# Plain pair of the second network: earlier weight loads, six split buffers, an even spread of the output layer and of the token work

## The chip, the cores and the metric

The kernel runs on one core of one Trainium2 chip. The metric is the device time of one execution, in microseconds (us). A core has five engines, each with its own in-order instruction stream: PE (matmul; PEld is its weight load), DVE (vector), ACT (scalar, reads PSUM), POOL (GpSimd, cannot read PSUM) and SP, which here only issues DMAs. A DMA waits on SP for its own conditions, and everything queued behind it on SP waits too.

## The reference

Three stages follow each other: a WKV recurrence over 768 steps (4 batches, 8 heads of 48), a first network and a second network. The change lies in the second one and at its border to the first:

```
# x: 3072 tokens x 384, from the recurrence
h = x @ w_in                              # 384 -> 2048
x = (h * clip(h + 3, 0, 6) / 6) @ w_out   # first network, 2048 -> 384
rms = sqrt(mean(x * x, axis=-1) + 1e-6)
xn = x / rms * rms_g
g = xn @ w_gate                           # second network, 384 -> 1536
silu = g / (1 + exp(-g))
return (silu * (xn @ w_val)) @ w_out      # 1536 -> 384
```

## The kernel before

The 3072 tokens are cut into six chunks of 512. The first network runs chunk by chunk, 16 steps of 128 hidden features each (`steps`); the recurrence and the preparation of weights run beside it. Each chunk's normalised result goes to DRAM (`xn`). The second network takes the chunks as three **pairs** p = 0, 1, 2. Its 1536 hidden features are four groups of 3 x 128; each group takes two **periods**, one for the gate and one for the value, so a pair has eight periods and the loop variable `j` runs from 0 to 24 (24 flushes). `p, k = divmod(j, 8)`.

Every fp32 factor is split into a high and a low fp32r part (copy on ACT, subtraction on POOL or DVE), and every product is three matmuls of 128x512 (`triple`, line 729 before, 730 after the change): high-high, high-low, low-high. Such a threesome is called a **unit** below, and the order of all engines' instructions is pinned to the order in which the program writes them (`pin`).

Pair 0 is the **plain pair** (`Plain`, j = 0 to 7): 18 units a period, three per hidden tile, with the weights `wp` that are loaded into two slots (`slots[0]` is the tile `w0`, printed as `w`; `slots[1]` is the front of `wide_b`). The other two pairs (`Triple`) form the 3x3 by 3x2 block product with 15 products in place of 18, from combinations of weights (`wd`) and of tokens. Both kinds of combination are made beside the plain pair, as **chores** placed at unit counts: `Group.sums` adds weight planes (DVE, line 226), `Group.split` splits five pieces per group into `chl` buffers (ACT line 249, POOL line 250) and stores them to DRAM as `wd`; `Combined.add` forms token combinations (`xc`, POOL line 693) and `Combined.split` splits them into their homes in `wide_a` and `wide_b` (`part`, ACT line 711, POOL or DVE line 712). For pair 2 the token work runs inside the last three periods of pair 1 and the first of pair 2, through the queue `after(n, ...)`, which runs a function n units later.

In a gate period ACT writes silu; in a value period DVE (plain) or POOL (`Triple`; for the product e6 DVE) multiplies with the gate (`done`, lines 826 and 829) and ACT and POOL split the result for the output layer (lines 834 and 835, tiles `xt` and `g`). The output layer's units (`out_units`, nine per chunk and group, result `o`) are a list `fill` that is interleaved with the period's own units; in `Triple` periods the letter F of `FULL` takes one. PSUM results of the plain pair rotate over four banks (`pa`, `pc`, `pe`, `pb`).

SP's stream before: `load_wp(0)` stands after the first network, `load_wp(j + 1)` at the start of period j, `load_wo` (output weights) in odd periods, `load_wc`/`load_we` (the combined weights, in two parts) for pairs 1 and 2, and between them the `wd` stores and the loads of `planes`.

Of the kernel before, what the change touches and what calls it, by code (L numbers as in the profile page):

```python
# [10 lines left out]
F32R = mybir.dt.float32r  # L11
# [24 lines left out]
def kernel(  # L36
# [171 lines left out]
    class Group:  # L208
# [36 lines left out]
        def split(self, b):  # L245
            hl = pl_p.tile([128, 2 * DM], F32R, tag="hl", name="chl", bufs=3)
            h = hl.rearrange("p (i l n) -> p i l n", i=3, l=2)
            a = planes[:, 9 + 3 * b:12 + 3 * b, :]
            nc.scalar.activation(out=h[:, :, 0, :], in_=a, func=AF.Copy)  # L249
            nc.gpsimd.tensor_tensor(out=h[:, :, 1, :], in0=a, in1=h[:, :, 0, :].bitcast(F32), op=ALU.subtract)  # L250
            nc.sync.dma_start(out=wd_d[self.j][:, 768 * b:768 * b + 768], in_=hl.bitcast(F32))
# [493 lines left out]
    class Triple:  # L745
# [76 lines left out]
        def done(self, i, o, ps=None):  # L822
# [13 lines left out]
            after(2, split)  # L836
# [119 lines left out]
    for n, (c, f, cols) in enumerate(steps):  # L956
# [15 lines left out]
        if n == first[NC_ - 1]:  # L972
# [4 lines left out]
            built = Combined(0)  # L977
        run(before[n])
# [36 lines left out]
    xwork = [start_x1, cut(10), add("6"), add("4"), add("44"), add("9"), cut(8), add("7"), add("0"), cut(6)]  # L1015
    xwork += [add("12"), cut(7), cut(4), add("13"), cut(12), add("11"), cut(13), add("3"), cut(14), add("1"), cut(11)]
    chores = {}
    for i, g in enumerate(groups):
        for n in range(4):
            chores.setdefault(24 * i + 2 + 2 * n, []).append(lambda g=g, n=n: g.sums(n))  # L1020
        for n in range(5):
            chores.setdefault(24 * i + 11 + 3 * n, []).append(lambda g=g, n=n: g.split(n))
        if i > 1:
            for n in range(4):
                if xwork:
                    chores.setdefault(24 * i + 3 + 2 * n, []).append(xwork.pop(0))
    assert not xwork
# [14 lines left out]
    load_wp(0)  # L1042
    for j in range(6 * NG + 1):
        p, k = divmod(j, 2 * NG)
        if j < 6 * NG:
            if j < 7:
                load_wp(j + 1)
            elif j + 1 < 6 * NG:
# [13 lines left out]
        else:  # L1062
            cur = None
        if k == 5 and 0 < p < NC_ // 2 - 1:
            coming = Combined(p + 1)
            for i, o in enumerate(coming.FIRST):
                after(9 + 2 * i, add(o))
        if j > 2:
            p2, k2 = divmod(j - 3, 2 * NG)
            fill += out_units(p2, k2 // 2, k2 % 2, (0, 1, 2), None if cur else ("a", "b", "c"))  # L1070
        if j < 8:
            for x in cur.units((0, 1)):
                paced(x)
                if fill:
# [5 lines left out]
        for u in FULL if cur else FLUSH:  # L1080
            if u == "F":
                unit(fill.pop(0))
            elif u[0] == "e" and u != "e1":
                if prev:
                    unit(lambda: prev.product(u))
                    if k == 0 and coming:
                        q = CHAIN[u][2]
                        after(0, lambda q=q, x=coming: x.split(q))
            else:
                unit(lambda: cur.product(u))  # L1090
                if k == 2 * NG - 1 and coming:
                    q = CHAIN[u][2]
                    after(0, lambda q=q, x=coming: x.split(q, q in (10, 6, 4, 13)))
                    for o in {7: ("13",), 4: ("11",), 14: ("3", "1")}.get(q, ()):
                        after(0, lambda o=o, x=coming: x.add(o))
# [88 lines left out]
```

## Time and profile before

| what | value |
|---|---|
| runs | 1009.23 us median of 3 (1008.8 to 1011.26) |
| profiled execution | 1010.94 us, of it a span of 1009.1 us from first to last instruction |
| PE busy | 957.4 us, 5097 matmuls |
| DVE, ACT, POOL busy | 660.7, 460.1, 533.3 us |
| mean granted PE clock | 0.979 of 2.4 GHz |
| DMA | 186.34 MB, mean 185 GB/s |

The profiled execution is 1.84 us longer than its span, and 1.71 us above the median of the runs. The first network ends and the second begins at 537.45 us of the span; the plain pair ends near 705 us, pair 1 near 861 us. PE is the busiest engine, so what counts is PE's idle time and the stretches in which its clock is at the lower level; idle time of other engines counts only where PE waits for them in the end.

### The profile page before, as it was taken

How to read it: one execution, taken by the hardware profiler on the slowest of the kernel's cores; microseconds unless marked ns; L12 is line 12 of the kernel's file. 1: busy time of each engine (PE TensorE's matmuls, PEld its weight loads, DVE VectorE, ACT ScalarE, POOL GpSimd, SP SyncE). 2: the span in 40 equal slices, each digit the busy share in tenths (PEclk: the TensorE clock that was granted, in tenths of full speed). 3: DMA queues.
4: the chain of work that ended last, by engine and by line, in shares of the span. 5: the costliest groups of instructions: out<-in, count | busy, mean ns of one | idle time of the engine just before them, and what ended most of it. 6: DMA issues, size and time to landing. Idle time of an engine off the chain costs nothing. (4 is left out here: it accounts for less than half of the span.)

```text
span 1009.1 us, 14229 instructions
## 1 busy us (share of the span) xinstructions
PE 957.4 (95%) x5097; PEld 745.9 (74%) x5097; DVE 660.7 (65%) x897; ACT 460.1 (46%) x905; POOL 533.3 (53%) x454
## 2 busy tenths in 40 slices
PE   5899999999999999999996987989999989999998
PEld 4675457778878877877875766867788867788876
DVE  7878857787878778876782535574545447554553
ACT  3545446656545645564652532334443334433331
POOL 0033315766766856774673556786253486255335
PEclk9799999999999999999997998989999999999999
DMA  9587632246536545454655575857644542462421
GB/s 347 181 318 258 236 124 81 91 152 231 187 114 218 206 148 199 152 168 165 207 191 195 188 267 176 286 193 263 230 154 180 227 163 79 162 228 90 193 73 63
DMA packets 62118, 186.34 MB, mean 185 GB/s; under 512 B 8800, under 2 KB 22496, under 8 KB 57440
## 3 DMA queue, kind: packets, MB, share of 16 engines
q1 hardware_dynamic: 62048, 185.44, 52.4%
q8 instruction: 40, 0.66, 0.3%
q14 instruction: 30, 0.25, 0.1%
HBM read 131.14 MB, written 44.04 MB: 174 GB/s over the span
## 5 line engine op out<-in xcount | busy, mean ns | idle before, releaser
L459 POOL TENSOR_TENSOR g<-a,g 128x512 fp32r<-128x512 f32 x80 | 112.2, 1403 | 126.1 <-ACT g L458 125.9
L729 PE MATMUL o<-xt,wide_b 128*128 128x512 f32 x405 | 111.8, 404 | 0.0
L465 PE MATMUL o<-g,wide_b 128*128 128x512 f32 x405 | 105.2, 402 | 0.3 <-POOL g L459 0.3
L436 PE MATMUL hps<-xt,wide_b 128*128 128x512 f32 x405 | 101.7, 395 | 0.0
L458 ACT ACTIVATE g<-a 128x512 fp32r<-128x512 f32 x80 | 50.6, 633 | 95.0 <-DVE a L454 88.8
L729 PEld LDWEIGHTS o<-xt,wide_b 128*128 128x128 f32 x405 | 78.6, 194 | 19.3
L436 PEld LDWEIGHTS hps<-xt,wide_b 128*128 128x128 f32 x405 | 75.9, 187 | 18.4
L465 PEld LDWEIGHTS o<-g,wide_b 128*128 128x128 f32 x405 | 75.2, 189 | 18.9 <-POOL g L459 0.7
L454 DVE SCALAR_TENSOR_TENSOR a<-a,hps 128x512 f32<-128x512 f32 x80 | 54.4, 681 | 46.8 <-ACT a L453 46.8
L453 ACT ACTIVATE a<-hps,half 128x512 f32<-128x512 f32 x80 | 54.5, 682 | 60.0 <-PE hps L436 53.9
L226 DVE TENSOR_TENSOR planes<-planes 128x256 f32<-128x256 f32 (+1 forms) x72 | 51.1, 758 | 44.3 <-POOL chl L250 38.4
L465 PE MATMUL o<-g,wide_a 128*128 128x512 f32 x315 | 78.7, 394 | 0.0
L436 PE MATMUL hps<-xt,wide_a 128*128 128x512 f32 x315 | 78.6, 394 | 0.0
L271 DVE TENSOR_TENSOR_SCAN w<-w,dd 128x520 f32<-128x520 f32 x48 | 72.5, 1510 | 4.5 <-DMA w<-in_dram 2.9
L436 PEld LDWEIGHTS hps<-xt,wide_a 128*128 128x128 f32 x315 | 59.1, 188 | 14.0 <-issue 1.2
L465 PEld LDWEIGHTS o<-g,wide_a 128*128 128x128 f32 x315 | 58.2, 188 | 12.3 <-issue 0.2
L829 POOL TENSOR_TENSOR o<-o,o 128x512 f32<-128x512 f32 x8 | 10.4, 1297 | 102.5 <-DVE o L764 81.4
L250 POOL TENSOR_TENSOR chl<-planes,chl 128x384 fp32r<-128x384 f32 x40 | 41.4, 1044 | 42.4 <-ACT chl L249 42.3
L329 ACT ACTIVATE a<-iperm,cb 128x128 f32<-128x128 f32 x192 | 58.5, 388 | 0.4 <-DVE cb L303 0.3
L764 DVE TENSOR_TENSOR q<-pc,q 128x512 f32<-128x512 f32 x64 | 44.2, 691 | 21.0 <-PE pc L729 10.6
L298 POOL TENSOR_TENSOR rks<-rks 128x384 f32<-128x384 f32 x20 | 30.2, 1510 | 52.1 <-DMA rks<-in_dram 40.1
L729 PE MATMUL o<-g,wide_b 128*128 128x512 f32 (+1 forms) x225 | 57.1, 386 | 0.5 <-DVE x L891 0.5
(193 smaller groups left out, 2085.0 us busy)
## 6 DMA issues: line engine op xcount, KB each, us to landing
wd<-chl SPq DMA_DIRECT2D x40, 384.0 KB, 4.5
wraw<-in_dram SPq DMA_DIRECT2D x36, 384.0 KB, 3.6
wide_b<-wo SPq DMA_DIRECT2D x12, 1152.0 KB, 9.3
w<-in_dram SPq DMA_DIRECT2D x24, 520.0 KB, 3.8
rk<-in_dram SPq DMA_DIRECT2D x24, 512.0 KB, 4.9
raw<-in_dram SPq DMA_DIRECT2D x16, 768.0 KB, 7.2
w<-wd SPq DMA_DIRECT2D x8, 1280.0 KB, 5.8
wide_b<-wd SPq DMA_DIRECT2D x8, 1280.0 KB, 6.0
```

Source lines behind the costliest of these rows:

```text
L226: nc.vector.tensor_tensor(out=two(*out), in0=two(*a), in1=two(*b), op=o)
L250: nc.gpsimd.tensor_tensor(out=h[:, :, 1, :], in0=a, in1=h[:, :, 0, :].bitcast(F32), op=ALU.subtract)
L271: nc.vector.tensor_tensor_scan(out=x, data0=x, data1=dd.rearrange("p a h j -> p (a h j)"), initial=0.0, op0=ALU.mult, op1=ALU.add)
L329: nc.scalar.activation(out=self.head(h), in_=iperm, func=AF.Copy, scale=self.cb[:, h, :])
L436: nc.tensor.matmul(ps, slot[:, l, k * 128:(k + 1) * 128], xt[:, k, r, :], start=(k == 0 and j == 0), stop=(k == KT - 1 and j == 2))
L453: nc.scalar.activation(out=a, in_=ps, func=AF.Relu, scale=1.0 / 6.0, bias=half)
L454: nc.vector.scalar_tensor_tensor(out=a, in0=a, scalar=1.0, in1=ps, op0=ALU.min, op1=ALU.mult)
L458: nc.scalar.activation(out=g[:, 0, :], in_=a, func=AF.Copy)
L459: nc.gpsimd.tensor_tensor(out=g[:, 1, :], in0=a, in1=g[:, 0, :].bitcast(F32), op=ALU.subtract)
L465: nc.tensor.matmul(acc[m][:, cols], slot[:, l, m * 128:(m + 1) * 128], g[:, r, :], start=(first and j == 0), stop=(parts or last and j == ...
L729: nc.tensor.matmul(ps, lhs[:, l, :], rhs[:, r, :], start=first and j == 0, stop=True, skip_group_check=not (first and j == 0))
L764: nc.vector.tensor_tensor(out=out, in0=a, in1=b, op=op)
```

## The change

It does six things. (1) `load_wp(0)` moves to the start of chunk 5 of the first network, `load_wp(1)` to its step 13; the other weight loads stay at the start of the period before their use. (2) `split` rotates over six buffers in place of three: four `chl` tiles and two pieces of the weight slots (columns 2560 to 3327) that the plain pair does not fill. (3) The sums and splits of a weight group stand later and further apart (splits every 2.5 units in place of 3, but 6 units ahead of the next sums in place of 3). (4) The load of the next pair's tokens and its twenty pieces of token work move: the load to count 24, the work to periods 2, 4 and 6, every three units, and five of the subtractions from POOL to DVE. (5) The output layer of a group starts one period earlier (j = 2), with eight units spread over each period's 18 instead of one after each of its first nine; six of them are left for j = 8, which had nine. (6) In pairs 1 and 2 the split of a value product is queued four units after it instead of two, the token splits two units after the product that frees their home instead of none; pair 2's tokens are loaded at k = 4 and added from unit 2 of k = 5, before: loaded at k = 5, added from unit 9; two more of pair 2's subtractions go to POOL.

```diff
--- before.py
+++ after.py
@@ -243,7 +243,8 @@
                     groups[self.j + 1].load()
 
         def split(self, b):
-            hl = pl_p.tile([128, 2 * DM], F32R, tag="hl", name="chl", bufs=3)
+            n = (5 * self.j + b) % 6
+            hl = slots[n][:, 2560:3328] if n < 2 else pl_p.tile([128, 2 * DM], F32R, tag="hl", name="chl", bufs=4)
             h = hl.rearrange("p (i l n) -> p i l n", i=3, l=2)
             a = planes[:, 9 + 3 * b:12 + 3 * b, :]
             nc.scalar.activation(out=h[:, :, 0, :], in_=a, func=AF.Copy)
@@ -833,7 +834,7 @@
                 g = gset(self.j // 2 * 2 + t)[f]
                 nc.scalar.activation(out=g[:, 0, :], in_=o, func=AF.Copy)
                 nc.gpsimd.tensor_tensor(out=g[:, 1, :], in0=o, in1=g[:, 0, :].bitcast(F32), op=ALU.subtract)
-            after(2, split)
+            after(4 if self.fast else 2, split)
 
     class Plain(Triple):
 
@@ -975,6 +976,9 @@
             slots = [f_p.tile([128, 15 * 256], F32R, name="w0"), wide_b[:, 0:3840]]
             xr_p = pool(ctx, "xr", side="left", reuse_waits="tile")
             built = Combined(0)
+            load_wp(0)
+        if n == first[NC_ - 1] + 13:
+            load_wp(1)
         run(before[n])
         if c == NC_ - 1:
             for i, x in ((0, 4), (2, 5), (4, 6), (5, 7), (1, 15)):
@@ -1012,19 +1016,18 @@
     def cut(q, pool=True):
         return lambda: coming.split(q, pool)
 
-    xwork = [start_x1, cut(10), add("6"), add("4"), add("44"), add("9"), cut(8), add("7"), add("0"), cut(6)]
-    xwork += [add("12"), cut(7), cut(4), add("13"), cut(12), add("11"), cut(13), add("3"), cut(14), add("1"), cut(11)]
+    xwork = [cut(10), add("6"), add("4"), add("44"), add("9"), cut(8, False), add("7"), add("0"), cut(6, False)]
+    xwork += [add("12"), cut(7), cut(4, False), add("13"), cut(12, False), add("11"), cut(13), add("3")]
+    xwork += [cut(14), add("1"), cut(11, False)]
     chores = {}
     for i, g in enumerate(groups):
         for n in range(4):
-            chores.setdefault(24 * i + 2 + 2 * n, []).append(lambda g=g, n=n: g.sums(n))
+            chores.setdefault(24 * i + 6 + 2 * n, []).append(lambda g=g, n=n: g.sums(n))
         for n in range(5):
-            chores.setdefault(24 * i + 11 + 3 * n, []).append(lambda g=g, n=n: g.split(n))
-        if i > 1:
-            for n in range(4):
-                if xwork:
-                    chores.setdefault(24 * i + 3 + 2 * n, []).append(xwork.pop(0))
-    assert not xwork
+            chores.setdefault(24 * i + 14 + 5 * n // 2, []).append(lambda g=g, n=n: g.split(n))
+    chores.setdefault(24, []).append(start_x1)
+    for n, x in enumerate(xwork):
+        chores.setdefault((42, 94, 146)[n // 7] + 3 + 3 * (n % 7), []).append(x)
     count = 0
 
     def paced(x):
@@ -1039,13 +1042,12 @@
     FLUSH = "e2 F F e3 F F e4 F F e5 F e6 F F".split()
     prev, gate, coming = None, None, None
     fill = ff2_units() + ff2_units()
-    load_wp(0)
     for j in range(6 * NG + 1):
         p, k = divmod(j, 2 * NG)
         if j < 6 * NG:
-            if j < 7:
+            if 0 < j < 7:
                 load_wp(j + 1)
-            elif j + 1 < 6 * NG:
+            elif j > 6 and j + 1 < 6 * NG:
                 load_wc(j + 1)
             if j > 7:
                 load_we(j)
@@ -1061,17 +1063,21 @@
             gate = cur if k % 2 == 0 else None
         else:
             cur = None
+        if k == 4 and 0 < p < NC_ // 2 - 1:
+            coming = Combined(p + 1)
         if k == 5 and 0 < p < NC_ // 2 - 1:
-            coming = Combined(p + 1)
             for i, o in enumerate(coming.FIRST):
-                after(9 + 2 * i, add(o))
-        if j > 2:
+                after(2 + 2 * i, add(o))
+        if 1 < j < 8:
+            fill += out_units(0, j // 2 - 1, j % 2, (0, 1, 2))
+        elif j > 8:
             p2, k2 = divmod(j - 3, 2 * NG)
             fill += out_units(p2, k2 // 2, k2 % 2, (0, 1, 2), None if cur else ("a", "b", "c"))
         if j < 8:
-            for x in cur.units((0, 1)):
+            room = 8 if j else 18
+            for i, x in enumerate(cur.units((0, 1))):
                 paced(x)
-                if fill:
+                if fill and i * room // 18 < (i + 1) * room // 18:
                     paced(fill.pop(0))
             continue
         if j == 8:
@@ -1079,20 +1085,21 @@
                 after(2 + 2 * i, lambda q=q, x=coming: x.split(q, q in (1, 0, 5)))
         for u in FULL if cur else FLUSH:
             if u == "F":
-                unit(fill.pop(0))
+                if fill:
+                    unit(fill.pop(0))
             elif u[0] == "e" and u != "e1":
                 if prev:
                     unit(lambda: prev.product(u))
                     if k == 0 and coming:
                         q = CHAIN[u][2]
-                        after(0, lambda q=q, x=coming: x.split(q))
+                        after(2, lambda q=q, x=coming: x.split(q))
             else:
                 unit(lambda: cur.product(u))
                 if k == 2 * NG - 1 and coming:
                     q = CHAIN[u][2]
-                    after(0, lambda q=q, x=coming: x.split(q, q in (10, 6, 4, 13)))
+                    after(2, lambda q=q, x=coming: x.split(q, q in (10, 6, 7, 4, 13, 11)))
                     for o in {7: ("13",), 4: ("11",), 14: ("3", "1")}.get(q, ()):
-                        after(0, lambda o=o, x=coming: x.add(o))
+                        after(2, lambda o=o, x=coming: x.add(o))
         if k == 0:
             coming = None
         prev = cur
```

What the built programs' order shows at three places. **SP**, around the end of the first network (`w0` and `wide_b` are the two slots, `wp0` and `wp1` their weights, `wo3` and `xn4` stores of the first network, `planes` the first weight group). Before:

```order
L206 DMA wo3_146<-hl_5058 128x768
L206 DMA wo3_146<-hl_5093 128x768
L516 DMA xn4_117<-x1_4628 128x1536
L215 DMA planes_5165<-wx0_135 128x1152
L662 DMA w0_4551<-wp0_127 128x2304
L662 DMA wide_b_634<-wp1_128 128x2304
L215 DMA planes_5165<-wx1_136 128x1152
```

After the change, the same place:

```order
L206 DMA wo3_146<-hl_5059 128x768
L663 DMA wide_b_634<-wp1_128 128x2304
L206 DMA wo3_146<-hl_5095 128x768
L517 DMA xn4_117<-x1_4629 128x1536
L215 DMA planes_5167<-wx0_135 128x1152
L215 DMA planes_5167<-wx1_136 128x1152
```

`wp1` moved ahead of two stores and of `planes`; `wp0` is no longer here, it stands 35 places further up, behind the two loads of chunk 5's token tiles.

**PE**, the start of period 2 (`pa` to `pb` are the plain pair's own units, `o` the output layer). Before:

```order
L729 MATMUL pa<-wide_a,w_4551 128x512 x9
L729 MATMUL pc<-wide_a,w_4551 128x512 x9
L729 MATMUL pe<-wide_a,w_4551 128x512 x9
L729 MATMUL pb<-wide_b,w_4551 128x512 x6
L729 MATMUL pb<-wide_a,w_4551 128x512 x3
```

After:

```order
L730 MATMUL pa<-wide_a,w_4551 128x512 x9
L730 MATMUL o_5436<-xt,wide_b 128x512 x3
L730 MATMUL pc<-wide_a,w_4551 128x512 x6
L730 MATMUL o_5436<-xt,wide_b 128x512 x3
L730 MATMUL pc<-wide_a,w_4551 128x512 x3
L730 MATMUL pe<-wide_a,w_4551 128x512 x3
L730 MATMUL o_5436<-xt,wide_b 128x512 x3
```

Period 2 has no output units before and eight after; before, period 3 is the first with any.

**POOL**, where pair 2's tokens are added beside pair 1's value products (`xc` the additions, line 829 or 830 the product with the gate, line 835 or 836 its split). Before:

```order
L693 TENSOR_TENSOR xc_6847<-xc_6847,xraw_6843 128x512 x2
L829 TENSOR_TENSOR o1_6948<-o1_6948,o1_6823 128x512
L835 TENSOR_TENSOR xt_5393<-o1_6948,xt_5393 128x512
L829 TENSOR_TENSOR q2_6869<-q2_6869,q2_6742 128x512
L835 TENSOR_TENSOR xt_5340<-q2_6869,xt_5340 128x512
```

After:

```order
L694 TENSOR_TENSOR xc_6709<-xc_6709,xraw_6705 128x512 x2
L830 TENSOR_TENSOR o1_6935<-o1_6935,o1_6814 128x512
L830 TENSOR_TENSOR q2_6856<-q2_6856,q2_6731 128x512
L836 TENSOR_TENSOR xt_5392<-o1_6935,xt_5392 128x512
L836 TENSOR_TENSOR xt_5341<-q2_6856,xt_5341 128x512
```

The split of a product now stands behind the next product instead of directly behind its own.

## Rows read from the trace of the kernel before

**Rows 1.** The page: an engine's busy time, share of the span, instructions.

```profile
PE 957.4 (95%) x5097; PEld 745.9 (74%) x5097; DVE 660.7 (65%) x897; ACT 460.1 (46%) x905; POOL 533.3 (53%) x454
```

**Rows 2.** Windows by stage; columns in the first line.

```profile
core 0: us, PE busy (x) PEld busy (x) DVE busy (x) ACT busy (x) POOL busy (x), PEclk, DMA share, GB/s
0.00:537.45 537.45, 520.00 (x3268) 397.98 (x3268) 422.55 (x553) 285.13 (x592) 290.63 (x260) 0.99 0.55 188
537.45:705.48 168.03, 146.24 (x589) 115.67 (x588) 81.24 (x121) 60.26 (x118) 101.36 (x86) 0.92 0.65 231
705.48:800.00 94.52, 94.08 (x404) 75.78 (x405) 48.88 (x71) 37.81 (x65) 35.10 (x28) 1.00 0.53 200
800.00:870.00 70.00, 62.56 (x257) 48.32 (x256) 40.01 (x54) 30.60 (x55) 50.18 (x37) 0.98 0.36 136
```

**Rows 3.** Timeline of PE, plain pair: start, us, instruction, [idle before <-releaser].

```profile
545.99 1.62 PE L729 MATMUL pa<-wide_a,w 128*128 128x512 f32 x3 [8.54 <-DVE planes L226]
...
550.88 0.85 PE L729 MATMUL pa<-wide_a,w 128*128 128x512 f32 x3
...
594.96 1.62 PE L729 MATMUL pe<-wide_a,wide_b 128*128 128x512 f32 x3 [2.66 <-DMA wide_b<-wp]
...
598.62 0.86 PE L729 MATMUL o<-xt,wide_b 128*128 128x512 f32 x3
...
621.09 1.65 PE L729 MATMUL pa<-wide_a,w 128*128 128x512 f32 x3 [5.56 <-DVE a L829]
...
625.99 0.86 PE L729 MATMUL pa<-wide_a,w 128*128 128x512 f32 x3
...
664.15 1.65 PE L729 MATMUL pa<-wide_a,w 128*128 128x512 f32 x3 [3.14 <-DVE a L829]
...
670.36 0.86 PE L729 MATMUL o<-xt,wide_b 128*128 128x512 f32 x3
```

**Rows 4.** Timeline of PE, end of pair 1 and start of pair 2.

```profile
812.75 0.96 PE L729 MATMUL pc<-wide_b,w 128*128 128x512 f32 x3 [1.13 <-DVE q L764]
...
825.89 0.96 PE L729 MATMUL pe<-wide_b,w 128*128 128x512 f32 x3 [2.65 <-DVE o L764]
...
831.03 0.86 PE L729 MATMUL pe<-wide_a,w 128*128 128x512 f32 x3
```

**Rows 5.** Timeline of SP: two issues of plain weights.

```profile
538.44 0.86 SPq L662 DMA_DIRECT2D w<-wp  x1
...
587.26 0.79 SPq L662 DMA_DIRECT2D wide_b<-wp  x1
```

**Rows 6.** Line 662, the eight loads of plain weights.

```profile
DMA to landing us min/median/max: 6.3/7.4/9.3
```

**Rows 7.** Timelines of ACT and DVE, before the wait at 621 us.

```profile
615.94 0.52 ACT L249 ACTIVATE chl<-planes 128x384 fp32r<-128x384 f32 x1 [7.27 <-DMA wd<-chl]
...
617.57 2.87 DVE L226 TENSOR_TENSOR planes<-planes 128x256 f32<-128x256 f32 x2 [11.76 <-POOL chl L250]
```

**Rows 8.** Timeline of POOL: third value split of period 1.

```profile
578.34 1.34 POOL L835 TENSOR_TENSOR xt<-a,xt 128x512 fp32r<-128x512 f32 x1
```

**Rows 9.** Timeline of DVE: weight sums with POOL idle, then busy.

```profile
543.12 2.97 DVE L226 TENSOR_TENSOR planes<-planes 128x256 f32<-128x256 f32 x9 [5.60 <-DMA planes<-wx]
...
636.03 6.49 DVE L226 TENSOR_TENSOR planes<-planes 128x256 f32<-128x256 f32 x6 [3.59 <-POOL chl L250]
```

**Rows 10.** Lines: DVE product with the gate; token subtraction on POOL and on DVE.

```profile
L829 DVE TENSOR_TENSOR s<-pe,s 128x512 f32<-128x512 f32 x8 | 5.4, 677 | 9.6 <-PE pe L729 9.6
...
L712 POOL TENSOR_TENSOR wide_a<-xc,wide_a 128x512 fp32r<-128x512 f32 x7 | 9.8, 1404 | 5.3 <-ACT wide_a L711 5.3
L712 DVE TENSOR_TENSOR wide_a<-xc,wide_a 128x512 fp32r<-128x512 f32 x5 | 6.9, 1371 | 2.7 <-ACT wide_a L711 2.7
```

**Rows 11.** Timelines of POOL and ACT, end of pair 1.

```profile
800.38 2.54 POOL L693 TENSOR_TENSOR xc<-xraw 128x512 f32<-128x512 f32 x2 [11.89 <-DMA xraw<-xn]
...
823.94 0.63 ACT L834 ACTIVATE xt<-q 128x512 fp32r<-128x512 f32 x1 [2.63 <-POOL q L829]
```

## Prediction

> **What bounds it.** The page comes first: PE is busy for 957.4 of 1009.1 us, far above the others [rows 1], so time is to be had only where PE stands idle or runs at the lower of its two clock levels. The windows by stage say where. The plain pair (537.45 to 705.48) has 168.03 us with 146.24 us of PE and a granted clock of 0.92; the first part of pair 1 has 94.52 with 94.08 at 1.00; the stretch from 800 to 870 has 70.00 with 62.56 at 0.98 [rows 2]. So PE idles 21.79, 0.44 and 7.44 us there, 29.7 us in all, nearly all of it in two stretches that the change rewrites. Of its other idle time 17.45 us lie before 537.45 [rows 2], which the change leaves alone but for two loads. The stretch at full clock also gives the price of a matmul: 94.08 us for 404, 0.233 us, so a unit of three is 0.70 us.
>
> The timeline of PE names four large waits in the plain pair: 8.54 us before the first unit, 2.66 at 594.96, 5.56 at 621.09, 3.14 at 664.15 [rows 3]. They make 19.90 of the 21.79; the rest (1.89) is short ones. After each, PE runs at the lower level (1.2 GHz) for a while, and the rows at which full pace is back are shown: 12 matmuls from 545.99 to 550.88, where 2.80 us were due, so 2.09 are lost; 9 up to 598.62, 1.56 lost; 12 up to 625.99, 2.10; 15 up to 670.36, 2.71 [rows 3]. That is 8.46 us. At the end of pair 1 the waits are smaller (1.13 at 812.75 and 2.65 at 825.89 are shown, four others make the rest of 7.44), and the largest costs clock too: 15 matmuls from 825.89 to 831.03, 5.14 us in place of 3.50, 1.64 lost [rows 4]. All this together is 29.7 + 8.46 + 1.64 = 39.8 us. The profiled execution took 1010.94, so with none of it left it would take 971.1: the floor, since the change adds no matmul.
>
> **Part by part.** *The first two weight loads.* `w` was issued at 538.44, after the first network [rows 5]; loads of this line land 6.3 to 9.3 us after their issue, 7.4 in the middle [rows 6], and 538.44 + 7.4 is where PE starts. The DVE name in PE's row is only the last event of that moment. The change issues this load a whole chunk earlier, and the second one about two steps before the end of the first network. Gain 8.54 + 2.09 = 10.6 us. Next late are the planes, at 543 us, on which DVE alone waits. What the load costs where it goes: at most its 0.86 us on SP [rows 5] and 1.2 MB of transfer (the tile is 128x2304 fp32) under the matmuls of chunk 5, a stretch in which the DMA engines are half busy [rows 2]; I take nothing. If that cover were gone, 7.4 us would come back once. Period 1 needs the second load after period 0's 24 units, 16.8 us.
>
> *The wait at 594.96.* Its load went out at 587.26 [rows 5], queued on SP behind stores of splits that POOL had not finished. It was late by 2.66 us. Period 2 now has 26 units in place of 18, 5.6 us more cover, so even the same late issue would be in time. Gain 2.66 + 1.56 = 4.2 us.
>
> *The waits at 621 and 664.* A chain ends in them: ACT waited 7.27 us for a store to free a split buffer, POOL's subtraction came after it, DVE sat 11.76 us until POOL had read the planes, then did two sums (2.87 us), and the gate product for which PE held a bank stood behind those [rows 7]. Three buffers came round after nine units, 6.3 us; six come round after 24, 16.8 us, so a store as slow as this one is covered; and the last split stands six units (4.2 us) before the next sums. Gain 5.56 + 2.10 + 3.14 + 2.71 = 13.5 us. What stays behind is DVE's own load, below.
>
> *Output layer.* The number of its units is the same; period 8 has six of them in place of nine, and the plain pair nine more. Its first unit comes in period 2 and needs period 1's splits: the third of them was done at 578.34 + 1.34 = 579.7 [rows 8], 33.7 us after the first unit, 31.6 without the clock loss; the unit that needs it is number 51 now, 35.7 us after the start. So 4 us in hand. It also needs output weights, asked for at the start of period 1, 14.7 us ahead. No row shows them under this traffic: at the 9.3 us of rows 6 they wait for nothing; if they and the other loads asked for there (3.9 MB by the tiles' shapes) got only the stage's mean of 231 GB/s [rows 2] they would take 17.0 us and PE would wait 2.3. I take 0, by the nearest row. Period 8 is three units shorter; its own successor's weights then have 16 units, 11.2 us, against 9.3. Two products on one bank stand one unit apart there, not two: 0.4 us, an estimate from the 0.68 us of DVE's read-out less what a unit covers, and twice at most.
>
> *Chores on DVE.* Nine sums of a group took 2.97 us while POOL rested and six took 6.49 beside a busy POOL [rows 9]: 0.33 or 1.08 us each. With POOL's work spread evenly I take the dear price throughout. A period of 26 units (18.2 us) then has 9.75 sums, 10.5 us. In value periods six gate products and three output additions at 0.68 come to it [rows 10]: 16.6 us. In gate periods three additions and up to three token subtractions at 1.37: 16.7 us. Both are under 18.2, and a bank that is read late has 13 units of reserve, so no wait is charged. POOL gives five subtractions of 1.40 us away [rows 10].
>
> By the Trainium skill (SBUF — State Buffer, Who interferes with whom) a DVE instruction with two SBUF inputs and a GpSimd instruction that reads SBUF exclude each other, and the one that comes second waits for the whole of the other. The trace agrees in direction, 0.33 against 1.08 us [rows 9]. Going by that rule alone, moving subtractions to DVE frees nothing while POOL runs, and this part would be worth 0 or less; it is rival B below.
>
> *End of pair 1.* POOL's additions began at 800.38 only, 11.89 us idle for the token load [rows 11], and ran into the value products; then ACT stood behind POOL (2.63 us at 823.94) while PE needed a bank copied by ACT [rows 11]. The load is now asked for a period (24 units, 16.8 us) earlier and the split is two units (1.4 us) later, behind the next product, so ACT meets a finished POOL. POOL's work in that period is the same. Of the 7.44 + 1.64 us I count 7 as gained; two subtractions more on POOL (2.8 us) at the end of the period are why not all. From below, the gain is 0 or, if those two delay every product of the next period by 2.8 us, a loss of that size.
>
> *Sum.* 10.6 + 4.2 + 13.5 + half of the short waits (0.9) + 7 - 0.4 = 35.8 us, and 1010.94 - 35.8 gives 975.1; I say **975.0**. The profiled execution was 1.71 us above the median of its runs, which the lower end allows for.
>
> **Rivals.** *A: the chain of rows 7 stays.* If POOL, not the buffers, is what is late, the sums wait as before and 13.5 us come back: 988.5. For it: POOL is busy 101 of 168 us there [rows 2]. Against: ACT's wait names the store. *B: DVE becomes the bound.* If sums beside POOL cost more than 1.08 us, value periods pass 18.2 us (1.25 us each is enough) and the gate products of periods 3, 5 and 7 come late, each like the wait at 664 with its clock: 3 x 5.85 = 17.6, 992.6. *C: the end of pair 1 is not cured:* 7 us come back, 982.0. *D: slower.* SP works in order, and each plain weight load stands behind up to five stores that wait for POOL. If POOL falls behind evenly, every load goes out late; the point is 18.2 - 9.3 = 8.9 us into its period. Each period start would then wait like the first, 8.54 + 2.09; four of them eat the gain, all eight give 975 + 85 = 1060. For it: 587.26 was such an issue. Against: one of eight loads was late, and by 2.66. *E: the change does not do what it says,* for instance because a piece of a weight slot used as a buffer makes the weight load wait for its store, and PE starts late as before: within 3 us of 1009.
>
> **Numbers.** Forecast (971 to 979) 0.62; C 0.14; A 0.10; B 0.08; D 0.04; E 0.02. The range goes from 969.5 (the floor less 1.6 for a run like the median's) to 986.0, which takes in C and the milder half of A and leaves out B, D and E: about 0.8. No change, within 0.3% (3 us, about what a measurement of this kernel can tell), is E: 0.02; slower is D: 0.04; faster the rest: 0.94.
>
> **What would show it.** Right: PE goes from the first network's last unit into the first plain unit without a gap over 1 us; the granted clock of the plain pair is 1.00; no ACT wait for a `wd` store; DVE's longest wait for POOL under 4 us; POOL's additions for pair 2 end before the gate products start. Wrong: a wait of PE over 2.5 us on DVE at the start of a value period's successor (A if DVE idled for POOL before it, B if DVE was busy), on a DMA at a period's start (D), or the waits between 800 and 870 still there, moved earlier with the rest (C).

## The result and the profile after

The changed kernel takes 972.82 us (median of four runs, 971.54 to 973.57) where the kernel before takes 1009.08 (1008.8 to 1011.26, four runs with it): a ratio of 0.9635, 95% interval 0.9617 to 0.9653; the medians differ by 36.3 us. The profiled execution took 971.54 us, with a span of 969.7.

The page of the changed kernel, the counterpart of [rows 1]:

```profile
PE 944.7 (97%) x5097; PEld 738.2 (76%) x5097; DVE 656.8 (68%) x900; ACT 460.8 (48%) x905; POOL 530.0 (55%) x451
```

PE does the same number of matmuls in 12.7 us less, as it spends less time at its lower clock: the mean granted clock rose from 0.979 to 0.996. The windows by stage, cut at the same places of the program as [rows 2] as nearly as a row allows (columns as there):

```profile
0.00:537.00 537.00, 519.65 (x3271) 397.68 (x3272) 422.04 (x553) 285.59 (x592) 290.90 (x261) 0.99 0.57 193
537.00:676.50 139.50, 139.35 (x601) 112.24 (x600) 81.12 (x126) 61.76 (x118) 97.63 (x83) 1.00 0.74 266
676.50:768.00 91.50, 90.97 (x392) 72.94 (x391) 48.22 (x70) 36.75 (x64) 41.77 (x33) 1.00 0.53 199
768.00:836.00 68.00, 65.62 (x279) 51.56 (x278) 40.77 (x56) 32.52 (x58) 43.78 (x32) 1.00 0.41 155
```

The first network is as it was. In the plain pair PE's idle time went from 21.79 us to 0.15 and the granted clock from 0.92 to 1.00; at the end of pair 1 the idle time went from 7.44 us to 2.38. The timeline of PE shows the border, the starts of periods 2 and 3, and all that is left of waits up to 836 us:

```profile
536.39 0.85 PE L730 MATMUL pa<-wide_a,w 128*128 128x512 f32 x3
537.09 0.86 PE L466 MATMUL o<-g,wide_b 128*128 128x512 f32 x3
...
566.18 2.22 PE L730 MATMUL pa<-wide_a,w 128*128 128x512 f32 x9
...
584.21 2.26 PE L730 MATMUL pe<-wide_a,wide_b 128*128 128x512 f32 x9
...
675.10 0.96 PE L730 MATMUL pb<-wide_a,w 128*128 128x512 f32 x3 [0.15 <-DVE a L830]
...
679.96 0.96 PE L730 MATMUL pc<-wide_a,w 128*128 128x512 f32 x3 [0.44 <-DVE q L765]
...
813.43 0.97 PE L730 MATMUL pe<-wide_a,wide_b 128*128 128x512 f32 x3 [0.78 <-DVE q L765]
...
820.59 0.96 PE L730 MATMUL pe<-wide_a,wide_b 128*128 128x512 f32 x3 [1.16 <-DVE q L765]
...
826.07 0.96 PE L730 MATMUL pe<-wide_b,w 128*128 128x512 f32 x3 [0.35 <-DVE o L765]
```

The first plain unit starts at 536.39 with no gap, among the last output units of the first network (line 466). None of the four large waits of [rows 3] has a successor, and of [rows 4] three waits of at most 1.16 us are left. The lines for the sums and for the copies into `chl`, to hold against [rows 7] and [rows 9] (busy us, mean ns of one | idle before, by releaser):

```profile
L226 DVE TENSOR_TENSOR planes<-planes 128x256 f32<-128x256 f32 (+1 forms) x72 | 42.3, 638 | 13.5 <-DMA planes<-wx 6.8 <-POOL chl L251 6.5
...
L250 ACT ACTIVATE chl<-planes 128x384 fp32r<-128x384 f32 x26 | 13.0, 512 | 4.6 <-DVE planes L226 4.6
```

These are 26 of the 40 copies; the other 14 go into the pieces of the weight slots. No copy waits for a `wd` store any more. DVE waits 6.5 us in all for POOL's chain, where one wait alone took 11.76 [rows 7]; the longest is now 4.59 (DVE's timeline):

```profile
578.56 9.14 DVE L226 TENSOR_TENSOR planes<-planes 128x256 f32<-128x256 f32 x9 [4.59 <-POOL chl L251]
```

For the experiments one more number is read from each profile: the length of the **second network**, from the end of the first network's matmuls to the end of the span. It was 1009.1 - 537.45 = 471.65 us before and 969.7 - 536.39 = 433.31 after. Where PE waits for the first plain weights, it is counted from the start of that wait. Nine profiles of kernels that are alike up to this border reach it anywhere between 536.39 and 539.60 us, so this number is free of a scatter of some 3 us that the whole time has. It comes from one profile of each kernel. In the four kernels below whose times agree with the changed kernel's it lies between 432.38 and 433.38, so a difference under 1 us in it is not read as an effect.

### The profile page after: what moved, and what is told of

It is laid out like the page before. It is cut to its first block, busy times and chain, and to the rows that moved or that the text cites. A ratio compares the mean times of both kernels' runs of the same rounds, so it can differ in the third digit from the quotient of the medians.

```text
span 969.7 us, 14234 instructions
## 1 busy us (share of the span) xinstructions
PE 944.7 (97%) x5097; PEld 738.2 (76%) x5097; DVE 656.8 (68%) x900; ACT 460.8 (48%) x905; POOL 530.0 (55%) x451
## 4 chain that ended last, share of the span: by engine, by line
PE 81%; DVE 8%; ACT 4%; issue 3%; DMA 2%; POOL 2%; SPq 1%; ACTq 0%; DVEq 0%; POOLq 0%
PE o L730 14%; PE o L466 12%; PE hps L437 12%; PE pe L730 9%; PE pc L730 8%; PE pa L730 5%; PE o L449 4%; PE hps L443 4%; PE pb L730 4%; PE aps L349 2%; PE yps L391 2%; DVE w L272 1%; ACT a L330 1%; DVE a L455 1%; PE yps L385 1%
## 5 line engine op out<-in xcount | busy, mean ns | idle before, releaser
L730 PE MATMUL o<-xt,wide_b 128*128 128x512 f32 x405 | 108.5, 395 | 0.0
L730 PEld LDWEIGHTS o<-xt,wide_b 128*128 128x128 f32 x405 | 76.0, 188 | 18.3
L226 DVE TENSOR_TENSOR planes<-planes 128x256 f32<-128x256 f32 (+1 forms) x72 | 42.3, 638 | 13.5 <-DMA planes<-wx 6.8
L830 POOL TENSOR_TENSOR q<-q,q 128x512 f32<-128x512 f32 x32 | 41.9, 1312 | 15.3 <-DVE q L765 15.3
```

The costliest lines, as they stand in the source:

```text
L226: nc.vector.tensor_tensor(out=two(*out), in0=two(*a), in1=two(*b), op=o)
L730: nc.tensor.matmul(ps, lhs[:, l, :], rhs[:, r, :], start=first and j == 0, stop=True, skip_group_check=not (first and j == 0))
L830: eng.tensor_tensor(out=o, in0=src, in1=self.gate.o[i], op=ALU.mult)
```

## The experiments

Each kernel is the changed kernel with one part undone, or the kernel before with one part added; runs of the kernel before on the same chip go with each, and the ratio is to those.

**The first two weight loads back behind the first network.**

```diff
-            load_wp(0)
-        if n == first[NC_ - 1] + 13:
-            load_wp(1)
...
+    load_wp(0)
     for j in range(6 * NG + 1):
-            if 0 < j < 7:
+            if j < 7:
                 load_wp(j + 1)
```

> The changed kernel with the two first weight loads back behind the first network. My theory (each term stands by itself): PE waits 8 to 9 us before the first plain unit again and runs about 12 matmuls at the lower clock, 10.6 us in all, so about 983.4 us against 972.8. Rival (PE would have found another wait at that place, for the planes or for a PSUM bank, so that the early load is worth little alone, or the later start is caught up by other covers): 973 to 977 us.

Measured: 982.66 us (981.84 to 983.04), ratio 0.9738 (0.9716 to 0.9760); the second network 443.96, 10.65 more. The timeline of PE has the old wait back, and this time its releaser is named as the load:

```profile
544.58 1.62 PE L730 MATMUL pa<-wide_a,w 128*128 128x512 f32 x3 [8.54 <-DMA w<-wp]
```

The term of 10.6 us stands, wait and clock together (one profile of each kernel; the medians differ by 9.8 us).

**Three buffers in the changed kernel.**

```diff
-            n = (5 * self.j + b) % 6
-            hl = slots[n][:, 2560:3328] if n < 2 else pl_p.tile([128, 2 * DM], F32R, tag="hl", name="chl", bufs=4)
+            hl = pl_p.tile([128, 2 * DM], F32R, tag="hl", name="chl", bufs=3)
```

> The changed kernel with three split buffers in place of six, the spacing of the chores kept. My theory (the buffers are what kept ACT waiting): ACT waits for stores again by 20 us or more in all, DVE waits for POOL, and PE's waits at the value periods' ends come back at least in part: 978 to 986 us. Rival (the spacing of the splits and their distance to the next sums do it, the buffers are of no use): ACT's waits for stores come back, but PE does not notice, 972 to 974 us.

Measured: 972.67 us (971.89 to 974.27), ratio 0.9642 (0.9619 to 0.9665); the second network 432.9. My theory falls: nothing came back. The lines show that the late part of the chain did come back all the same:

```profile
L226 DVE TENSOR_TENSOR planes<-planes 128x256 f32<-128x256 f32 (+1 forms) x72 | 46.3, 693 | 28.1 <-POOL chl L250 22.4 <-DMA planes<-wx 5.5
...
L249 ACT ACTIVATE chl<-planes 128x384 fp32r<-128x384 f32 x40 | 20.4, 518 | 43.9 <-DMA wd<-chl 27.2 <-DVE planes L226 11.5 <-issue 3.9
```

ACT waits 27.2 us for stores and DVE 22.4 for POOL, yet PE waits 0.15 us at the end of the plain pair and 0.44 at the start of pair 1, as with six buffers. The stores are still late; PE no longer stands behind them in time. DVE's timeline, and PE's where it takes the bank of the 5.56 us wait [rows 3] again:

```profile
601.43 1.83 DVE L226 TENSOR_TENSOR planes<-planes 128x256 f32<-128x256 f32 x2 [5.46 <-POOL chl L250]
603.19 0.68 DVE L829 TENSOR_TENSOR a<-pa,a 128x512 f32<-128x512 f32 x1
...
605.63 2.24 PE L729 MATMUL pa<-wide_a,w 128*128 128x512 f32 x9
```

DVE waits 5.46 us for POOL here, where it was 11.76 [rows 7], and is done with `pa` at 603.87, 1.76 us before PE takes it.

**Six buffers alone, in the kernel before** (the same edit the other way round).

> The kernel before with six split buffers in place of three and nothing else. My theory: ACT's waits for stores go (31.9 us in the trace of before), the chain that ends in the waits of 5.56 and 3.14 us of PE goes with them, and with their clock loss 13.5 us are gained: about 995.6 us. Rival (spacing is what counts: the sums come three units after the last split and wait for POOL with any number of buffers): 1004 to 1009 us.

Measured: 993.19 us (992.77 to 995.17), ratio 0.9847 (0.9824 to 0.9871); the second network 455.49, 16.2 less than before. The waits of 5.56 and 3.14 us are gone, and the load's wait before period 3 shrank from 2.66 us to 1.28. The timeline of PE:

```profile
592.58 0.94 PE L730 MATMUL pe<-wide_a,wide_b 128*128 128x512 f32 x3 [1.28 <-DMA wide_b<-wp]
```

So six buffers do cure the chain where nothing else is changed, and in the changed kernel they do nothing. Something else there cures it too. The next four runs look for it.

**Three buffers and the old places of the sums and splits, in the changed kernel.**

```diff
-            chores.setdefault(24 * i + 6 + 2 * n, []).append(lambda g=g, n=n: g.sums(n))
+            chores.setdefault(24 * i + 2 + 2 * n, []).append(lambda g=g, n=n: g.sums(n))
         for n in range(5):
-            chores.setdefault(24 * i + 14 + 5 * n // 2, []).append(lambda g=g, n=n: g.split(n))
+            chores.setdefault(24 * i + 11 + 3 * n, []).append(lambda g=g, n=n: g.split(n))
```

(and the edit to three buffers as above)

> The changed kernel with three split buffers and the old places of the weight sums and splits (sums 2 to 8 units, splits 11 to 23 units after the group's start). With three buffers alone nothing was lost, though ACT waited 27.2 us for stores. Theory S (the new places kept PE out of it): the chain reaches PE again, 978 to 986 us. Rival R (the even spread of the output units and of the token work, which gives each PSUM bank more time, is what keeps PE out of it): 972 to 975 us, with ACT and DVE waiting as long as in the kernel before.

Measured: 976.88 us (974.65 to 978.37), ratio 0.9685 (0.9660 to 0.9709); the second network 437.16, 3.85 more than after the change. It lies between the two, and its largest wait is a new one, at the start of pair 1 (timeline of PE):

```profile
686.29 0.96 PE L729 MATMUL pc<-wide_a,w 128*128 128x512 f32 x3 [2.35 <-DVE q L764]
```

So the new places are not all that makes the buffers superfluous: with three buffers they are worth these 3.85 us, and most of the gain survives without both.

**The new places alone, in the kernel before** (the same four lines the other way round).

> The kernel before with only the new places of the weight sums and splits (splits every 2.5 units, six units ahead of the next sums); three buffers, all else as before. If the distance to the next sums is enough by itself, the 13.5 us of the chain go: 993 to 998 us. If a store that lands late still reaches PE through three buffers, because the period has no cover: 1002 to 1008 us.

Measured: 1007.27 us (1004.39 to 1010.76, ten runs), ratio 0.9985 (0.9971 to 0.9999); the second network 470.36, 1.3 less. The places alone move the waits and remove almost nothing. PE's timeline:

```profile
592.22 0.93 PE L729 MATMUL pe<-wide_a,wide_b 128*128 128x512 f32 x3 [2.58 <-DMA wide_b<-wp]
...
633.26 1.84 PE L729 MATMUL pc<-wide_b,w 128*128 128x512 f32 x6 [3.74 <-ACT s L826]
...
657.97 1.22 PE L729 MATMUL pa<-wide_a,w 128*128 128x512 f32 x3 [1.93 <-DVE a L829]
...
705.56 1.06 PE L729 MATMUL pc<-wide_a,w 128*128 128x512 f32 x3 [2.91 <-DVE q L764]
```

Behind the wait of 3.74 us stands a store again, now by way of ACT. ACT's timeline:

```profile
632.20 0.52 ACT L249 ACTIVATE chl<-planes 128x384 fp32r<-128x384 f32 x1 [5.02 <-DMA wd<-chl]
632.63 0.58 ACT L826 ACTIVATE s<-pc 128x512 f32<-128x512 f32 x1
```

The copy waits 5.02 us for its buffer, and the read-out of the bank `pc` that PE needs stands behind it.

**The even output layer alone, in the kernel before.**

```diff
-        if j > 2:
+        if 1 < j < 8:
+            fill += out_units(0, j // 2 - 1, j % 2, (0, 1, 2))
+        elif j > 8:
...
-            for x in cur.units((0, 1)):
+            room = 8 if j else 18
+            for i, x in enumerate(cur.units((0, 1))):
                 paced(x)
-                if fill:
+                if fill and i * room // 18 < (i + 1) * room // 18:
                     paced(fill.pop(0))
...
             if u == "F":
-                unit(fill.pop(0))
+                if fill:
+                    unit(fill.pop(0))
```

> The kernel before with only the output layer's new place (from period 2 on, eight units spread over each period, six left for period 8); three buffers, old chore places, old loads. The changed kernel with three buffers and old chore places lost only 4 us, so the even spread of the output units may be what keeps PE out of the chain. Theory R (it is): the load wait with its clock (4.2 us) and most of the 13.5 us of the chain go, 992 to 997 us. Theory S (the token work at its old, crowded places still makes DVE and POOL late): only the load wait goes, 1002 to 1006 us.

Measured: 1001.37 us (998.97 to 1001.72), ratio 0.9921 (0.9903 to 0.9939), between the two expectations. ACT still waits 24.9 us for stores in it, but PE does far less so. PE's timeline, after the first wait of 8.53 us:

```profile
617.40 1.66 PE L729 MATMUL pc<-wide_a,w 128*128 128x512 f32 x6 [0.50 <-DVE s L829]
...
649.83 0.96 PE L729 MATMUL pb<-wide_b 128*128 128x512 f32 x3 [2.19 <-DVE s L829]
...
699.03 1.65 PE L729 MATMUL pc<-wide_a,w 128*128 128x512 f32 x3 [3.12 <-DVE q L764]
```

The load's wait is gone and those of 5.56 and 3.14 have become 0.50 and 2.19; one of 3.12 us appears where pair 1 begins. Its profiled run is its shortest, 2.4 us under the median, so I take the median: 7.7 us less than before. The second network of that profile, 460.24, is 11.4 less.

**The output layer back to its old place, in the changed kernel** (the same lines the other way round, but for the guard at F, which stays).

> The changed kernel with the output layer back at its old place (first units in period 3, one after each of the first nine units of a period, nine left for period 8); six buffers and the new chore places kept. Theory (the early and even output layer is a cover for late DVE work, not a gain of its own): with six buffers nothing is late, so 972 to 975 us; at most the 1.7 us of two load waits that six buffers alone on the kernel before still had. Rival (the long rows of own units without output units between make PE wait for DVE): 976 to 985 us, with PE waits on DVE in periods 1 to 7.

Measured: 979.04 us (978.57 to 979.56), ratio 0.9710 (0.9694 to 0.9726); the second network 438.91, 5.6 more. The size is in the rival's range, but the wait is not the one that it named. PE's timeline:

```profile
568.17 2.21 PE L730 MATMUL pa<-wide_a,w 128*128 128x512 f32 x9
...
584.71 1.07 PE L730 MATMUL pe<-wide_a,wide_b 128*128 128x512 f32 x3 [3.96 <-DMA wide_b<-wp]
...
681.41 0.96 PE L730 MATMUL pb<-wide_a,w 128*128 128x512 f32 x3 [0.78 <-DVE a L830]
```

And the issue of that load, SP's timeline of this kernel:

```profile
575.54 0.38 SPq L663 DMA_DIRECT2D wide_b<-wp  x1
```

SP's timeline of the changed kernel, at the same place:

```profile
573.13 0.32 SPq L252 DMA_DIRECT2D wd<-w  x1
573.55 0.38 SPq L663 DMA_DIRECT2D wide_b<-wp  x1
```

In both kernels the load for period 3 leaves 7.37 us after period 2 begins (568.17 and 566.18), queued behind a `wd` store. Here it needed 9.17 us to land, in a period of 18 units, 12.58 us: 3.96 late. In the changed kernel the period lasts 584.21 - 566.18 = 18.03 us, which leaves 1.5 us over for a load as slow as this one. The load is still late; the period is longer.

**The split of a product two units after it, in the changed kernel.**

```diff
-            after(4 if self.fast else 2, split)
+            after(2, split)
```

> The changed kernel with only the product split of pairs 1 and 2 back at two units after the product. Undoing all of the changes in pairs 1 and 2 cost 7.1 us. Theory (ACT standing behind POOL is the larger share, since the largest wait, 2.65 us, was on a bank copied by ACT): 977 to 979 us. Rival (the late token load is the share that counts): 973 to 974.5 us.

Measured: 980.84 us (978.29 to 981.33), ratio 0.9723 (0.9703 to 0.9743); the second network 440.62, 7.3 more. The timeline of all engines around the largest wait shows how:

```profile
813.96 1.29 POOL L830 TENSOR_TENSOR q<-q,q 128x512 f32<-128x512 f32 x1
815.28 0.63 ACT L835 ACTIVATE g<-q 128x512 fp32r<-128x512 f32 x1 [3.91 <-POOL q L830]
815.82 0.61 ACT L712 ACTIVATE wide_b<-xc 128x512 fp32r<-128x512 f32 x1
...
816.53 1.27 DVE L713 TENSOR_TENSOR wide_b<-xc,wide_b 128x512 fp32r<-128x512 f32 x1 [4.32 <-ACT wide_b L712]
817.72 0.68 DVE L765 TENSOR_TENSOR q<-pe,q 128x512 f32<-128x512 f32 x1
...
818.46 0.80 PE L730 MATMUL pe<-wide_a,wide_b 128*128 128x512 f32 x1 [3.83 <-DVE q L765]
```

The split's copy stands on ACT and waits 3.91 us for POOL's product. Behind it stands a token copy; DVE waits 4.32 for that copy, and behind DVE's subtraction stands the read of the bank that PE needs. In the changed kernel the token copy stands ahead of the split's, as ACT's timeline there shows:

```profile
811.01 0.64 ACT L712 ACTIVATE wide_b<-xc 128x512 fp32r<-128x512 f32 x1 [2.06 <-POOL xc L694]
812.26 0.63 ACT L835 ACTIVATE g<-q 128x512 fp32r<-128x512 f32 x1 [0.62 <-POOL q L830]
```

The token copy no longer stands behind POOL's product (it waits 2.06 us for POOL's addition), and PE's wait at this unit is 0.78 us (the row at 813.43) in place of 3.83.

**Pair 2's tokens loaded and added late again.**

```diff
-        if k == 4 and 0 < p < NC_ // 2 - 1:
-            coming = Combined(p + 1)
         if k == 5 and 0 < p < NC_ // 2 - 1:
+            coming = Combined(p + 1)
             for i, o in enumerate(coming.FIRST):
-                after(2 + 2 * i, add(o))
+                after(9 + 2 * i, add(o))
```

> The changed kernel with only pair 2's token load and additions back where they were (load at the start of period 5 of pair 1, additions from unit 9). Theory (the smaller share): POOL's additions run into the value products again, but ACT no longer stands behind POOL: 973.5 to 976 us. Rival (the larger share): 977 to 980 us.

Measured: 972.77 us (972.11 to 973.16), ratio 0.9647 (0.9631 to 0.9664); the second network 433.38, 0.07 more. POOL's timeline of this kernel, to hold against the 11.89 of [rows 11]:

```profile
769.81 2.54 POOL L694 TENSOR_TENSOR xc<-xraw 128x512 f32<-128x512 f32 x2 [10.39 <-DMA xraw<-xn]
```

POOL's wait is back, and with the splits where the change has them it costs nothing.

**All of the changes to pairs 1 and 2 undone**: the two edits above, and the token splits and the last additions right behind the product (`after(0, ...)` for `after(2, ...)`, and the old list `(10, 6, 4, 13)` of POOL's subtractions).

> The changed kernel with everything it does in pairs 1 and 2 undone (product splits two units later, token splits at once, pair 2's tokens loaded and added a period later, two subtractions back on DVE). My theory: the waits at the end of pair 1 come back, 7 us with their clock loss, 979.8 us. Rival (those waits came from the plain pair's delays and went with them): 972.5 to 974.5 us.

Measured: 979.89 us (979.45 to 980.72), ratio 0.9714 (0.9689 to 0.9740); the second network 440.56, 7.25 more. PE's timeline has the waits of [rows 4] back, one of them with the same 2.6 us:

```profile
781.34 0.96 PE L730 MATMUL pc<-wide_b,w 128*128 128x512 f32 x3 [1.12 <-DVE q L765]
...
794.48 0.97 PE L730 MATMUL pe<-wide_b,w 128*128 128x512 f32 x3 [2.63 <-DVE o L765]
```

The split alone (7.3) costs as much as the whole part (7.25). The waits do not lie alike, though: here four of the six over 1 us lie between 781 and 807 us (the other two, 1.08 and 1.37, at 830 and 834), with the split alone undone all three lie between 818 and 833. Two things differ between these kernels, the tokens' load and additions and the places of the token splits, and no run tells them apart. The later split removes the large waits with the tokens loaded early or late.

**The five subtractions back on POOL**: `cut(q)` for `cut(q, False)` with q = 8, 6, 4, 12 and 11.

> The changed kernel with the five token subtractions that it gave to DVE back on POOL. Theory (neither engine is the bound in the plain pair): 972 to 974 us. Rival (POOL's relief is needed): 976 us or more, with PE waits on DVE behind POOL. By the rule of the Trainium skill (SBUF - State Buffer, Who interferes with whom) the move frees nothing while both engines run; the time would be the same or a little lower, 970 to 973 us.

Measured: 972.63 us (972.14 to 972.93), ratio 0.9640 (0.9626 to 0.9655); the second network 432.85, 0.46 less. The line of the sums:

```profile
L226 DVE TENSOR_TENSOR planes<-planes 128x256 f32<-128x256 f32 (+1 forms) x72 | 49.2, 734 | 18.5 <-POOL chl L251 7.9 <-DMA planes<-wx 5.5 <-POOL w L251 2.9
```

A sum takes 734 ns in place of 638 with that work on POOL, so the two engines do slow each other, as the Trainium skill has it (SBUF — State Buffer, Who interferes with whom), by which the second of two such instructions waits for the whole of the first. The trace agrees, in size too. The lengths of the 72 sums fall into two groups, as the shortest, median and longest show (of the changed kernel, then of this one):

```profile
L226 DVE TENSOR_TENSOR planes<-planes x72: 273/417/1514, 543.4 to 664.5; 128x256 f32<-128x256 f32 x56, 128x128 f32<-128x128 f32 x16
...
L226 DVE TENSOR_TENSOR planes<-planes x72: 276/420/1517, 544.1 to 666.4; 128x256 f32<-128x256 f32 x56, 128x128 f32<-128x128 f32 x16
```

A sum takes 0.27 to 0.43 us, or 0.78 to 1.52 where a POOL instruction runs for at least 0.7 us of it; none lies between. There are 18 long ones in the changed kernel and 25 here, together 6.9 us more for five subtractions of 1.40 us (7.0) on POOL. None of it reaches PE.

**A try at the waits that are left**: pair 2's last two additions two products of `c` earlier (behind c3 in place of c5), its token splits in the first period of pair 2 two units later.

```diff
-                        after(2, lambda q=q, x=coming: x.split(q))
+                        after(4, lambda q=q, x=coming: x.split(q))
...
-                    for o in {7: ("13",), 4: ("11",), 14: ("3", "1")}.get(q, ()):
+                    for o in {7: ("13",), 4: ("11",), 13: ("3", "1")}.get(q, ()):
```

> A further step on the changed kernel: pair 2's last two additions two products earlier, and its last token splits four units after their product in place of two. Three waits of PE are left there (0.78, 1.16 and 0.35 us, on DVE, which waits for ACT, which waits for POOL's additions). Theory: the first goes and the second shrinks, 1 to 2.5 us gained, 970 to 972 us. Rival (POOL's products beside DVE's subtractions are what is late): no change within 1 us.

Measured: 971.85 us (971.24 to 972.53), ratio 0.9633 (0.9618 to 0.9648). The three waits after 800 us became two, 1.34 and 0.18 us, and the second network is 0.9 us shorter in the one profile; but the runs overlap those of the changed kernel and the two ratios agree within their intervals. That it beats the change is not shown.

## Why the prediction was right, and where its reasons were not

The forecast was 975.0 us with a likely case of 971 to 979; 972.82 lies in it. By the second network of the two profiles the gain is 38.3 us where the sum had 35.8.

- **First two loads, 10.6 us:** right, 10.65 when undone. The DVE name in PE's row of [rows 3] was indeed not the cause: undone, the same wait of 8.54 us names the load.
- **The wait at 594.96, 4.2 us by 26 units of cover:** right in mechanism, and closer than I thought. I counted 5.6 us more cover against a lateness of 2.66; the rows show 1.5 us in hand for a load as slow as the one in the run with the old output layer. Undone, it came back as 3.96 us, and 5.6 us of time.
- **The chain of [rows 7], 13.5 us:** the time was right, the step that named its cure was not. I wrote that six buffers that come round after 24 units cover the slow store, and that the new distance of the splits helps. Six buffers do it alone in the kernel before (16.2 us, with part of the load's wait), with POOL's work as it was, which answers rival A; in the changed kernel three do as well, with 27.2 us of store waits on ACT. The new places alone give 1.3 us. The even output layer alone turned 5.56 and 3.14 into 0.50 and 2.19, and so carries part of it without the buffers. I had booked it as cover for the weight load, and its 13 units as a reserve against DVE's own load, but not against this chain. The bank that PE needs first in a period (`pa` at 621.09 and 664.15) was last used as the third tile of the period before, and from there to its reuse lie nine units with the old output layer, all bare (6.3 us), and 13 with the even one (9.1 us): 2.8 us more for a late DVE. That is not the whole of it. At the first of the two places PE waited 5.56 us in the kernel before, and in the changed kernel with three buffers DVE was done 1.76 us early, 7.3 us between them; at the second it is 3.14 us of wait against 3.66 early (DVE done with `pa` at 638.18, PE there at 641.84), 6.8. Four units make 2.8 us of each; the rest is that DVE itself came earlier. Without the four units, on these rows, PE would have waited about 1 us at the first place and not at all at the second (an estimate). Which part of the change brings DVE forward stays open: no run had three buffers together with the old output layer and everything else new.
- **Output layer, 0 (at worst 2.3 for its own weights), and -0.4 for period 8:** the 0 is right; no PE wait in the plain pair names `wo`. The plain pair has three output units more (48 for 45), which are nine matmuls; "nine more" holds for matmuls, not units. The 0.4 did not show: the wait of 0.44 us where pair 1 begins (679.96) stands at the same place in the kernel before. PE's timeline there:

```profile
710.36 0.96 PE L729 MATMUL pc<-wide_a,w 128*128 128x512 f32 x3 [0.44 <-DVE q L764]
```

- **Sums at 1.08 us each:** too dear, 0.638 in the mean; the 1.08 was the mean of four sums of 1.50 to 1.52 us and two of 0.41. Since no wait had been charged for it, the sum didn't suffer. Rival B's condition, 1.25 us a sum, was not met: the mean is half of it.
- **End of pair 1, 7 us:** the size was right, 7.25 when undone, 7.3 for the later split alone. Half of its reason failed: the token load a period earlier, which I put first, is worth 0.07 us once the split is later, although it does remove POOL's wait of 11.89 us [rows 11]. Nor does ACT meet a finished POOL: its split copies still wait 11.0 us for POOL's products from 765 to 836 us, where it was 24.4 from 796 to 870. What changed, at the unit whose rows are shown above, is that the copy on which PE's bank hangs now stands ahead of the split's.
- **What I had not counted:** the short waits of the plain pair went nearly whole (1.74 of 1.89, where I took half), and PE's busy time fell by more than the 10.1 us of clock loss that I read after the large waits: 437.40 to 425.69 us over the second network, 11.7.

Undone one at a time, the first loads, the output layer and the end of pair 1 come to 10.65 + 5.6 + 7.25 = 23.5 of the 38.3 us. The rest goes mostly to the chain, where one cure stands in for another, so that undoing any one of them shows little.

Of the other rivals, C is what the run with pairs 1 and 2 undone gives (979.89 where I had 982.0). D is seen in small: the plain loads of the changed kernel leave 1.4 to 7.4 us into their period, the latest at 7.37, short of the 8.9 at which D begins. The markers came out as written, but for two: DVE's longest wait for POOL was 4.59 us where I wrote under 4, and two of POOL's additions, at 807.79 and 809.68, still run among the products.

## What to carry to other kernels

In this kernel a late load or store cost only what the matmuls in front of its user didn't cover, so ask first how many units the period has: eight units moved into it covered a load that was issued late, and gave a late chain 2.8 us. Where an in-order engine copies for two customers, put the copy that waits for a third engine behind the one that the bottleneck waits for; two units of distance were worth 7 us here. When several cures in a change meet the same wait, undoing one and doing one alone give different answers (0 and 16 us here for the buffers): run both before you say what a part is worth.

## What the runs showed that I had not expected

- The kernel ran with 27.2 us of ACT waiting for stores at the same time as with none (972.67 and 972.82 us).
- After a wait of the same length PE's next row was not always the same: behind 2.65 us at the same unit (`pe<-wide_b,w`, end of pair 1) three matmuls took 0.96 us in the kernel before [rows 4], 1.11 in the one with the even output layer alone and 1.65 in the one with the new places alone. So what a wait of this size costs in clock is read over the rows behind it, not from the first one.
- The plain weight loads took 5.5 to 9.3 us from issue to landing, median 7.7, nearly as before (6.3 to 9.3, 7.4), though the plain pair now moves 266 GB/s in place of 231.
